# Shared buffers, an eighth ring slot and one more resident key slice in a planned two-layer kernel

## The chip, the cores and the metric

The kernel runs on one core of a Trainium2 chip. The metric is the device time of one execution in microseconds (us). Below, PE is the matrix engine, "weight load" its separate instruction that brings in the stationary operand, DVE the vector engine, ACT the scalar engine, POOL the GpSimd engine, and SP the engine that here only issues DMA transfers.

## The reference

An input of 2048 tokens of 640 bf16 numbers goes through two kinds of layer in turn, A, B, A, B, with the same weights each time. Each layer works on the layer norm of its input and is added to it.

```python
def _A_ref(x, mem0, Wq, Wk, Wv, Wo, seg_len):      # 32 heads of 192, segments of 32 tokens
    mem = mem0                                      # 8 memory rows
    for s in range(n_seg):                          # 64 segments, one after the other
        h = concatenate([mem, x[segment s]])        # 40 rows
        q, k, v = h @ Wq, h @ Wk, h @ Wv            # 640 -> 32 x 192 each
        p = softmax(where(mask, q k^T * scale, -1e9))
        o = (p v) @ Wo                              # 6144 -> 640
        mem = o[:8]; outs.append(o[8:])

def _B_ref(x, w1, w2, w3, w4):
    h = gelu(layernorm(x) @ w1)                     # 640 -> 640, then four column groups are
    hs = shifted(h) @ w2                            # shifted by -1, +1, -2, +2 tokens
    x1 = x + hs
    return x1 + gelu(layernorm(x1) @ w3) @ w4       # 640 -> 1536 -> 640
```

The memory makes layer A a chain of 64 steps: a segment can't start before the one ahead of it has gone through all heads. The four projection weights have 640 x 6144 numbers each, 7.9 MB, and are needed anew in every step.

## The kernel before, in words

**Two lanes.** The second A layer follows the first five segments behind (`LAG`), so that one pass over the weights serves both: in step t lane 0 works on segment t of the first A layer, lane 1 on segment t - 5 of the second. There are 69 steps. In steps 5 to 63 both lanes run and a projection matmul has 80 columns (two times 40 rows); in the first and last five steps one lane runs and it has 40. A chunk of layer B, 64 tokens of both lanes, is spread over every second step.

**One step** has eight groups of four heads, taken in four pairs. For each pair `proj_pair` makes k, q and v of both groups (per group and kind 30 matmuls, 5 slices of the input dimension times 6 of the output), then `attend` runs for each group: scores (`pss`), mask and row minimum (DVE, L600), exponential (ACT, L607), row sums, reciprocal and scaling (DVE, L611 to L613), transposes of the probabilities (`pst`), their copy (ACT, `PT`), times V (`pso`), copy (DVE, `oT`) and the output projection, which adds into `psy`. At the end of a step ACT copies the new memory columns out of `psy` (L671), and the next step's projections wait for that.

**Weights.** The weights do not all fit in the core's memory. For each pair and kind some of the five slices are resident, loaded once by `res_tile`, and the others stream in every step: `STREAM` says 3 for k, 3 for q, 2 for v, that is 32 slices of 128 x 1536 bf16 (393,216 bytes) per step. They go through a ring of `RING_A = 7` slots (tiles `wst`, L440). A slot is free again after the second group's matmuls of its slice. Layer B's weights have a ring of their own (`wstB`, 3 slots). All these transfers are issued by SP, in one order.

**The planner.** The order of all instructions is made in Python when the kernel is built. Every operation is added with an engine, an assumed duration, a due time (48 us per step), and the buffers it reads and writes; the writes and reads of a named buffer `B(...)`, in the order of adding, give the dependencies. `Plan.place` then builds a list per engine: it always places the operation that can start first, and among those within a few hundredths of a microsecond the one due first. For a transfer it assumes a rate, `DMA_RATE`, and that data is there `DMA_LAST` after its last byte's turn; matmuls that read it are placed no earlier than that. A transfer may be put at most `DMA_AHEAD` in front of the transfer server; such a "paced" transfer gets a wait for the last matmul planned to be over by then. On the chip only the order and the waits remain: no assumed time is enforced.

**Buffers the change touches.** `qT`, `Pm` (two each, by group number) and `sm` (four) hold the queries, probabilities and softmax columns. `Vt` holds V of a group, each head padded from 192 to 256 columns. `mask2` and `mask_b` are fp32. In layer B `lnx` holds four rows of look-ahead and the next 64 input rows, `vT` the transposed normalised rows, `hTB` the transposed first hidden layer with four tokens of history, and `h2u` the second hidden layer.

Of the kernel before, what the change touches and what calls it, by code (L numbers as in the profile page):

```python
# [9 lines left out]
ACT = mybir.ActivationFunctionType  # L10
# [10 lines left out]
LAG = 5  # L21
HG = 4
STREAM = {"k": 3, "q": 3, "v": 2}
RING_A = 7
RING_B = 3
# [8 lines left out]
DMA_FIRST = 0.8  # L34
DMA_LAST = 2.6
B_MARGIN = 0.6
# [203 lines left out]
def kernel(  # L240
# [34 lines left out]
    NS = 2 * L1  # L275
    QD = Dm // 4
    scale = float(Dh) ** -0.5
    T_A = NSEG + LAG
# [33 lines left out]

    mask2 = ctile([NS, NS], f32, "mask2")
    nc.gpsimd.memset(mask2[:], 0.0)
# [11 lines left out]
    mask_a = mask2[0:L1, 0:L1]  # L326
    mask_b = ctile([L1, L1], f32, "mask_b")
    nc.gpsimd.memset(mask_b[:], 0.0)
# [11 lines left out]
    hT = [ctile([P, KC, NS], bf16, f"hT{i}") for i in range(4)]  # L340
    qT = [ctile([P, GC, NS], bf16, f"qT{i}") for i in range(2)]
    vF = ctile([P, GC, NS], bf16, "vF")
    kT = [ctile([P, 8, NS], bf16, f"kT{i}") for i in range(2)]
    Vt = [ctile([NS, HG, 256], bf16, f"V{i}") for i in range(2)]
    Pm = [ctile([NS, HG, NS], bf16, f"Pm{i}") for i in range(2)]
    PT = ctile([NS, HG, NS], bf16, "PT")
    oT = [ctile([P, GC, NS], bf16, f"oT{i}") for i in range(OT_BUFS)]
    sm = [ctile([P, 10], f32, f"sm{i}") for i in range(4)]
    mem0T = ctile([P, KC, M], bf16, "mem0T")
    yTB = ctile([P, KC, XB + 4], bf16, "yTB")  # L350
# [10 lines left out]
    gl = vbg[:].bitcast(f32)  # L361
    lnx = ctile([96, Dm], bf16, "lnx")
    vT = ctile([P, KC, XB + 4], bf16, "vT")
    hTB = ctile([P, KC, TOK + 4, 2], bf16, "hTB")
    st4 = [ctile([P, 18], f32, f"st{i}") for i in range(4)]

# [5 lines left out]
    nc.gpsimd.memset(xres[:], 0.0)  # L372
    nc.vector.memset(lnx[:], 0.0)
    nc.vector.memset(hTB[:], 0.0)

    bufs = {}
    ALIAS = {("vx",): ("vb",), ("xo",): ("vb",), ("gl",): ("vb",), ("vx2",): ("uw",), ("xres",): ("xw",)}

# [50 lines left out]
    def load_pair(kind, pr, due, now):  # L429

        nres = KC - STREAM[kind]
        cols = slice(PW * pr, PW * (pr + 1))
        rb, rt = res_tile((kind, pr), [P, nres, PW], w_src[kind][:, 0:nres, cols], due)
        slots = []
        for j, kc in enumerate(range(nres, KC)):
            b = Slotted("ra", None)
            b.make = lambda b=b: wring.tile([P, SLOT], bf16, name="wst", tag=f"ra{b.slot}")

            def fn(op, b=b, kc=kc):
                nc.sync.dma_start(out=T(b)[:, 0:PW], in_=w_src[kind][:, kc, cols])  # L440
# [57 lines left out]
    def attention_step(t):  # L498
# [13 lines left out]
        def proj_pair(pr):  # L512
            s0 = base + sl * 2 * pr
            for kind, off in (("k", 0.0), ("q", 0.2), ("v", 0.5)):
                wbs, wv = load_pair(kind, pr, s0 + off * 2 * sl, LEAD_A)
                for j in range(2):
# [4 lines left out]

                    nres = KC - STREAM[kind]
                    for kcs in [range(0, nres)] + [range(kc, kc + 1) for kc in range(nres, KC)]:
# [10 lines left out]
                    if kind == "q":  # L534
                        q = qT[G % 2]

                        def fq(op, pq=pq, q=q):
                            nc.scalar.copy(out=q[:, :, 0:N], in_=T(pq)[:, :, 0:N])  # L538
                        add("ACT", act_us(GC * N), due, fq, r=(pq,), w=(B("qT", G % 2),))
                    elif kind == "k":  # L540
# [13 lines left out]
                    else:  # L554
# [12 lines left out]
                        for hf in range(2):  # L567
                            def fe(op, pvt=pvt, V_=V_, hf=hf):
                                src = T(pvt)[0:N, GWH * hf:GWH * (hf + 1)].rearrange("n (a b) -> n a b", a=2)
                                dst = V_[0:N, 2 * hf:2 * hf + 2, 0:Dh]  # L570
                                if hf:
                                    nc.vector.tensor_copy(out=dst, in_=src)
                                else:
                                    nc.scalar.copy(out=dst, in_=src)  # L574
                            add("DVE" if hf else "ACT", dve_us(GWH) if hf else act_us(GWH), due, fe, r=(pvt,),
                                w=(B("V", G % 2, hf),))

        def attend(g):
            G = t * NG + g
            s0 = base + sl * g  # L580
            q, k_, V_ = qT[G % 2], kT[G % 2], Vt[G % 2]
            pss = ps("A", [NS, HG * NS], f32, "pss")
            hi = s0 + 0.5 * sl

            def fs(op):
# [6 lines left out]
            add("PE", mm_us(N, N, 4) + mm_us(2 * N, N, 2), hi - 4, fs,  # L592
                r=(B("qT", G % 2), B("kT", G % 2, 0), B("kT", G % 2, 1), B("kT", G % 2, 2)), w=(pss,))
            sm_ = sm[G % 4]
            Pb = Pm[G % 2]
            smk, Pk = B("sm", G % 4), B("P", G % 2)

# [12 lines left out]
            def f3(op):  # L610
# [3 lines left out]
                                        in1=sm_[0:N, 6:6 + HG].unsqueeze(2).to_broadcast([N, HG, N]), op=ALU.mult)  # L614
            add("DVE", 0.42 + 0.17 + 0.45, hi - 4, f3, w=(Pk, B("sm4", G % 4)))
            pst = ps("A", [NS, HG, NS], bf16, "pst")
# [11 lines left out]
            pso = ps("A", [P, GC, NS], f32, "pso")  # L628
            Vf = V_[:].rearrange("n h e -> n (h e)")

            def f6(op):
                o = T(pso)
                for hf in range(2):
                    for i2, col, c, st, sp in ((0, 0, 0, True, True), (0, 128, 1, True, False), (1, 192, 1, False, True),
                                               (1, 320, 2, True, True)):
                        nc.tensor.matmul(out=o[:, 3 * hf + c, 0:N], lhsT=Vf[0:N, 512 * hf + col:512 * hf + col + P],  # L636
                                         rhs=Pt[0:N, 2 * hf + i2, 0:N], start=st, stop=sp)
# [28 lines left out]
        if take:  # L666
# [5 lines left out]
            add("ACT", act_us(KC * (m1 - m0)), due, fm, r=(psy,), w=(mk,))  # L672
        if 1 in nxt and t + 1 == LAG:
            def fm0(op):
                nc.gpsimd.tensor_copy(out=hn[:, :, L1:L1 + M], in_=mem0T[:])
            add("POOL", 0.4, base, fm0, a=(mk,), r=(B("mem0T"),))
        t0 = 2 + SEG * (t % 2) if t < T_A - 1 else 2
# [85 lines left out]
    def chunk_loads(c, part):  # L763
        base = (2 * c + 1) * STEP
        edge = False
        todo = []
# [19 lines left out]
        if edge:  # L786
            def fz(op):
                nc.gpsimd.memset(xres[:] if part == "x" else lnx[0:4, :], 0.0)
            add("POOL", 1.0, base, fz, w=(B("xres") if part == "x" else B("lnx", "l"),))
        if part == "x":  # L790
            base = base + 0.6 * STEP
        for lane, a, b, w0 in todo if part == "x" else ():
# [4 lines left out]
        for lane, k0 in look if part == "l" else ():  # L797
            def f(op, lane=lane, k0=k0):
                nc.gpsimd.dma_start(out=lnx[lane:4:2, :], in_=src[lane][k0:k0 + 2, :])
            rd = [] if src[lane] is x0d else [B("x2d", k) for k in x2_chunks(k0, k0 + 2)]  # L800
            add("POOL", 0.9, base, f, r=rd, a=(B("lnx", "l"),), dma=4000)
        s = 2 * c + 4
        if s < NSEG and part == "l":
            def f(op):
                nc.gpsimd.dma_start(out=lnx[32:96, :], in_=x0d[SEG * s:SEG * s + TOK, :])
            add("POOL", 0.9, base, f, w=(B("lnx", "x"),), dma=TOK * Dm * 2)

# [4 lines left out]
    def chunk(c):  # L812
# [63 lines left out]
        add("DVE", 0.45, D(0.08), f3, r=(B("lnx", "l"), B("lnx", "x"), s2k), w=(vxk,))  # L876
        if c + 1 < NCH:
            chunk_loads(c + 1, "l")
        ps2 = ps(PB, [P, KC, XB], bf16, "psv")
# [51 lines left out]
        if last:  # L931
            def fc2(op):
                for r, r1, n, o2 in carry:
                    if o2:
                        nc.vector.tensor_copy(out=hTB[r:r1, n, 0:o2 // 2, 0], in_=hTB[r:r1, n, TOK:TOK + o2 // 2, 1])
            add("DVE", 0.6, D(0.4), fc2, w=(B("hTB", 0), B("hTB", 1)))
        hs = [ps(PB, [XB, HC], f32, "hs") for _ in range(2)]
        for i, (a, e) in enumerate(((0, 2), (2, 4), (4, 5))):
# [52 lines left out]
    def chunk_end(c):  # L991
# [56 lines left out]
    def start():  # L1048
# [10 lines left out]
        def f3(op):  # L1059
            nc.scalar.copy(out=mem0T[:], in_=T(p0)[:])  # L1060
            nc.scalar.copy(out=hT[0][:, :, SEG:L1], in_=T(p0)[:])
        add("ACT", 0.5, -90, f3, r=(p0,), w=(B("mem0T"), B("hT", 0, "m")))

# [80 lines left out]
```

## Time and profile before

| | |
|---|---|
| median of 3 runs | 3606.19 us (3599.22 to 3612.08) |
| span of the profiled execution | 3607.7 us |
| bytes moved by DMA | 1102.00 MB, mean 305 GB/s |
| chain that ended last | PE 73%, DMA 23%, issue 2% |
| slices streamed through the ring | 828 k, 828 q, 552 v |
| resident loads of k and q, of v, of the output weights | 8 of 768 KB, 4 of 1152 KB, 8 of 960 KB |
| mean granted PE clock | 0.981 of full |

How to read it: the profile gives each engine's busy time, and for the idle time of an engine what ended it, inferred from semaphores. PE work is pipelined: a matmul of 80 columns is recorded with 202 ns, but the next starts 36 ns after it, so records overlap, and a busy PE is counted until the last record ends. "PEld" are the weight loads, recorded with 100 ns each. A DMA is recorded at its issue on SP; the data lands microseconds later. "Issue" is idle time for which the profile has no releaser.

The granted clock is below full only in the first 300 us and the last 300 us of the run. Of the 40 slices of the page the first shows the PE busy 60% and the last 60%; nearly all between are at 90% or more.

### The profile page before, as it was taken

What the parts mean: (1) busy time and instruction counts of PE and PEld (TensorE: products, weight loads), DVE (VectorE), ACT (ScalarE), POOL (GpSimd) and SP (SyncE); (2) the same over time, 40 slices, a digit from 0 to 9 for tenths busy, and PEclk for the clock granted to TensorE, in tenths of its full rate; (3) what the DMA queues carried; (4) which work ended last, traced back from release to release, by engine and by line L of the source; (5) the groups of instructions that cost most, each with busy time, mean ns of one, the idle gap of its engine ahead of it and who ended that gap; (6) DMA issues with size and microseconds to landing.
All of it is one profiled execution on the core that took longest, in us unless ns stands there. A gap on an engine that the chain in (4) does not pass through costs nothing.

```text
span 3607.7 us, 187838 instructions
## 1 busy us (share of the span) xinstructions
PE 3398.0 (94%) x84559; PEld 3260.7 (90%) x84559; DVE 2484.8 (69%) x7432; ACT 1509.0 (42%) x3569; POOL 243.5 (7%) x456
## 2 busy tenths in 40 slices
PE   6899999999999999999999999999999999999886
PEld 5789999999999999999999999999999999999775
DVE  2556777777776777777767777777767777766554
ACT  1334444444444444444444444444444444444332
POOL 0000000000000000000000000000000000000000
PEclk7899999999999999999999999999999999999997
DMA  9899899888988898889888988888889888988995
GB/s 376 299 318 313 308 316 312 299 305 305 326 305 300 301 321 303 302 303 328 303 296 307 312 310 303 303 311 303 300 295 320 301 304 302 319 296 305 306 306 175
DMA packets 507559, 1102.00 MB, mean 305 GB/s; under 512 B 50558, under 2 KB 217996, under 8 KB 506752
## 3 DMA queue, kind: packets, MB, share of 16 engines
q1 hardware_dynamic: 499520, 1076.85, 86.1%
q8 instruction: 661, 10.83, 1.2%
q0 software_dynamic: 7232, 13.13, 1.1%
q14 instruction: 146, 1.20, 0.1%
HBM read 1084.53 MB, written 5.24 MB: 302 GB/s over the span
## 4 chain that ended last, share of the span: by engine, by line
PE 73%; DMA 23%; issue 2%; ACT 1%; DVE 1%; SPq 0%; POOL 0%; POOLq 0%; DVEq 0%; ACTq 0%
PE psy L653 15%; PE psq L528 13%; PE psv L528 12%; PE psk L528 12%; DMA wst<-in_A_Wq_dram 9%; DMA wst<-in_A_Wk_dram 9%; PE pvt L565 4%; PE pso L636 4%; PE pss L589 3%; DMA wst<-in_A_Wv_dram 3%; PE psh L982 3%; PE pst L621 2%; PE y L1008 2%; PE psh L910 1%; PE hs L947 1%
## 5 line engine op out<-in xcount | busy, mean ns | idle before, releaser
L528 PEld LDWEIGHTS <-wst 128*128 128x128 bf16 x26496 | 1087.7, 100 | 134.0 <-DMA wst<-in_A_Wq_dram 38.6
L653 PE MATMUL psy<-oT,wo 128*128 128x80 bf16 (+1 forms) x16560 | 678.4, 200 | 30.6 <-issue 17.4
L653 PEld LDWEIGHTS <-wo 128*128 128x128 bf16 x16560 | 619.0, 100 | 38.5 <-issue 25.8
L538 ACT CAST qT<-psq 128x480 bf16<-128x480 f32 (+1 forms) x552 | 283.7, 530 | 747.8 <-PE psq L528 746.2
L528 PE MATMUL psq<-hT,wst 128*128 128x80 bf16 (+1 forms) x9936 | 494.4, 199 | 29.4 <-DMA wst<-in_A_Wq_dram 24.6
L528 PE MATMUL psk<-hT,wst 128*128 128x80 bf16 (+1 forms) x9936 | 468.8, 200 | 31.5 <-DMA wst<-in_A_Wk_dram 25.6
L642 DVE CAST oT<-pso 128x480 bf16<-128x480 f32 (+1 forms) x552 | 340.7, 617 | 198.4 <-PE pso L636 195.9
L528 PE MATMUL psv<-hT,wv 128*128 128x80 bf16 (+1 forms) x9936 | 435.6, 200 | 14.2 <-DMA wv<-in_A_Wv_dram 7.3
L600 DVE CUSTOM_DVE_ANT_1 pss<-pss,mask 80x320 f32<-80x320 f32 (+1 forms) x512 | 245.1, 479 | 232.9 <-PE pss L589 216.0
L528 PEld LDWEIGHTS <-wv 128*128 128x128 bf16 x9936 | 383.4, 100 | 19.8 <-issue 8.0
L626 ACT COPY PT<-pst 80x320 bf16<-80x320 bf16 (+1 forms) x552 | 222.1, 402 | 367.4 <-PE pst L621 330.7
L574 ACT COPY V<-pvt 80x384 bf16<-80x384 bf16 (+1 forms) x552 | 261.2, 473 | 266.5 <-PE pvt L565 264.1
L528 PE MATMUL psv<-hT,wst 128*128 128x80 bf16 (+1 forms) x6624 | 350.7, 199 | 23.1 <-DMA wst<-in_A_Wv_dram 14.9
L611 DVE TENSOR_REDUCE sm<-Pm 80x4 f32<-80x320 bf16 (+1 forms) x552 | 250.3, 453 | 150.0 <-ACT Pm L607 146.3
L558 ACT CAST vF<-psv 128x480 bf16<-128x480 f32 (+1 forms) x552 | 290.9, 527 | 128.1 <-PE psv L528 127.1
L552 DVE CAST kT<-psk 64x160 bf16<-64x160 f32 (+1 forms) x1104 | 335.9, 304 | 9.4
L528 PE MATMUL psk<-hT,wk 128*128 128x80 bf16 (+1 forms) x6624 | 320.5, 200 | 15.7 <-ACT hT L671 10.7
L528 PE MATMUL psq<-hT,wq 128*128 128x80 bf16 (+1 forms) x6624 | 319.2, 200 | 2.5 <-issue 1.3
L607 ACT ACTIVATE Pm<-pss,sm 80x320 bf16<-80x320 f32 (+1 forms) x552 | 277.5, 505 | 81.5 <-DVE sm L600 81.0
L546 DVE CAST kT<-psk 128x320 bf16<-128x320 f32 (+1 forms) x552 | 255.3, 462 | 76.1 <-PE psk L528 67.3
L565 PE MATMUL pvt<-ident,vF 128*80 128x128 bf16 (+1 forms) x3312 | 284.7, 223 | 7.8 <-ACT vF L558 3.8
L528 PEld LDWEIGHTS <-wk 128*128 128x128 bf16 x6624 | 269.9, 100 | 22.8 <-issue 20.3
(126 smaller groups left out, 4345.3 us busy)
## 6 DMA issues: line engine op xcount, KB each, us to landing
wst<-in_A_Wk_dram SPq DMA_DIRECT2D x828, 384.0 KB, 5.2
wst<-in_A_Wq_dram SPq DMA_DIRECT2D x828, 384.0 KB, 5.1
wst<-in_A_Wv_dram SPq DMA_DIRECT2D x552, 384.0 KB, 5.0
wstB<-in_B_w_dram SPq DMA_DIRECT2D x495, 320.0 KB, 5.0
wstB<-in_B_w_dram SPq DMA_DIRECT2D x132, 160.0 KB, 4.8
wo<-in_A_Wo_dram SPq DMA_DIRECT2D x8, 960.0 KB, 12.3
wv<-in_A_Wv_dram SPq DMA_DIRECT2D x4, 1152.0 KB, 10.7
wk<-in_A_Wk_dram SPq DMA_DIRECT2D x4, 768.0 KB, 10.3
```

The costliest lines, as they stand in the source:

```text
L528: nc.tensor.matmul(out=o[:, cc, 0:N], lhsT=wv(kc, GW * j + cc * P, GW * j + (cc + 1) * P), rhs=h[:, kc, c0:c0 + N], start=(kc == 0 and cc ...
L538: nc.scalar.copy(out=q[:, :, 0:N], in_=T(pq)[:, :, 0:N])
L546: nc.vector.tensor_copy(out=k4[:, :, 0::3, 0:N], in_=p4[:, :, 0::2, 0:N])
L552: nc.vector.tensor_copy(out=k4[r0:r1, :, jj, 0:N], in_=p4[r0:r1, :, 1, 0:N])
L558: nc.scalar.copy(out=vf[:, :, 0:N], in_=T(pq)[:, :, 0:N])
L565: nc.tensor.transpose(out=o[0:N, c * P:(c + 1) * P], in_=vf[:, c, 0:N], identity=ident[:, :])
L574: nc.scalar.copy(out=dst, in_=src)
L600: nc.vector.tensor_tensor_reduce(out=o, in0=o, in1=maskt.unsqueeze(1).to_broadcast([N, HG, N]), scale=-scale, scalar=3.0e38, op0=ALU.add, ...
L607: nc.scalar.activation(out=Pb[0:N, :, 0:N], in_=o, func=ACT.Exp, bias=sm_[0:N, 0:1], scale=-1.0)
L611: nc.vector.tensor_reduce(out=sm_[0:N, 2:2 + HG], in_=Pb[0:N, :, 0:N], axis=AX.X, op=ALU.add)
L642: nc.vector.tensor_copy(out=o_[:, :, 0:N], in_=T(pso)[:, :, 0:N])
L653: nc.tensor.matmul(out=o[:, m, c0:c0 + N], lhsT=wo[:, cc, m * P:(m + 1) * P], rhs=o_[:, cc, 0:N], start=st, stop=True, skip_group_check=True)
```

## The change

It makes room by keeping fewer buffers, and spends the room on the ring and on residence.

- Room made: `qT` and `Pm` become single, `sm` two; the masks become bf16; `Vt` shares the padding between heads; `mem0T` goes (the first memory is copied straight to its place); `lnx` moves into columns of `h2u`, `vT` into `hTB`. As `hTB` is overwritten by `vT` in each chunk, its four tokens of history are saved to a small tile, `hist`, and put back. Loads into `lnx` now come at the end of a chunk, after the matmuls that read that part of `h2u`.
- Room spent: `RING_A` from 7 to 8; `MORE` keeps one more slice of k for pair 1, so that 31 slices stream per step.
- The plan: `DMA_LAST` from 2.6 to 3.2, so that matmuls are placed later relative to the transfers they read.

```diff
-RING_A = 7
+RING_A = 8
+MORE = {("k", 1): 1}
-DMA_LAST = 2.6
+DMA_LAST = 3.2
-    mask2 = ctile([NS, NS], f32, "mask2")
+    mask2 = ctile([NS, NS], bf16, "mask2")
-    mask_b = ctile([L1, L1], f32, "mask_b")
+    mask_b = ctile([L1, L1], bf16, "mask_b")
-    qT = [ctile([P, GC, NS], bf16, f"qT{i}") for i in range(2)]
+    qT = ctile([P, GC, NS], bf16, "qT")
-    Vt = [ctile([NS, HG, 256], bf16, f"V{i}") for i in range(2)]
-    Pm = [ctile([NS, HG, NS], bf16, f"Pm{i}") for i in range(2)]
+    Vt = [ctile([NS, 2 * VP], bf16, f"V{i}") for i in range(2)]
+    Pm = ctile([NS, HG, NS], bf16, "Pm")
-    sm = [ctile([P, 10], f32, f"sm{i}") for i in range(4)]
-    mem0T = ctile([P, KC, M], bf16, "mem0T")
+    sm = [ctile([P, 10], f32, f"sm{i}") for i in range(2)]
-    lnx = ctile([96, Dm], bf16, "lnx")
-    vT = ctile([P, KC, XB + 4], bf16, "vT")
+    lnx = h2u[0:96, Dm:2 * Dm]
     hTB = ctile([P, KC, TOK + 4, 2], bf16, "hTB")
+    vT = hTB[:].rearrange("p k w l -> p k (w l)")[:, :, 0:XB + 4]
+    hist = ctile([P, KC, 4, 2], bf16, "hist")
...
-        nres = KC - STREAM[kind]
+        nres = KC - STREAM[kind] + MORE.get((kind, pr), 0)
...
-                        q = qT[G % 2]
+                        q = qT
-                        add("ACT", act_us(GC * N), due, fq, r=(pq,), w=(B("qT", G % 2),))
+                        add("ACT", act_us(GC * N), due, fq, r=(pq,), w=(B("qT"),))
...
-        def fhh(op):
-            nc.gpsimd.tensor_copy(out=hTB[:, :, 0:4, :], in_=hTB[:, :, TOK:TOK + 4, :])
-        add("POOL", 0.4, D(0.05), fhh, w=(B("hTB", 0), B("hTB", 1)))
...
+        def fhr(op):
+            nc.gpsimd.tensor_copy(out=hTB[:, :, 0:4, :], in_=hist[:])
+        add("POOL", 0.6, D(0.25), fhr, r=(B("hist"),), w=(B("hTB", 0),))
...
+            def fhs(op):
+                nc.gpsimd.tensor_copy(out=hist[:], in_=hTB[:, :, TOK:TOK + 4, :])
+            add("POOL", 0.6, D(0.5), fhs, r=(B("hTB", 0),), w=(B("hist"),))
...
             chunk_loads(c + 1, "x")
+            chunk_loads(c + 1, "l")
```

More of the change, by code (lines that the diff above doesn't have):

```diff
@@ L276 @@
     QD = Dm // 4
+    VP = 2 * Dh + 64
     scale = float(Dh) ** -0.5
@@ L372 @@
     nc.gpsimd.memset(xres[:], 0.0)
-    nc.vector.memset(lnx[:], 0.0)
+    nc.vector.memset(lnx, 0.0)
+    nc.vector.memset(hist[:], 0.0)
     nc.vector.memset(hTB[:], 0.0)
     bufs = {}
-    ALIAS = {("vx",): ("vb",), ("xo",): ("vb",), ("gl",): ("vb",), ("vx2",): ("uw",), ("xres",): ("xw",)}
+    ALIAS = {("vx",): ("vb",), ("xo",): ("vb",), ("gl",): ("vb",), ("vx2",): ("uw",), ("xres",): ("xw",),
+             ("vTl",): ("vT",), ("hTB", 0): ("vT",), ("hTB", 1): ("vT",)}
     def B(*key):
@@ L520, in proj_pair @@
                     pq = ps("A", [P, GC, NS], f32, "ps" + kind)
-                    nres = KC - STREAM[kind]
+                    nres = KC - STREAM[kind] + MORE.get((kind, pr), 0)
                     for kcs in [range(0, nres)] + [range(kc, kc + 1) for kc in range(nres, KC)]:
@@ L569, in fe @@
                                 src = T(pvt)[0:N, GWH * hf:GWH * (hf + 1)].rearrange("n (a b) -> n a b", a=2)
-                                dst = V_[0:N, 2 * hf:2 * hf + 2, 0:Dh]
+                                v0 = hf * (VP - 64)
+                                dst = V_[0:N, v0:v0 + 512].rearrange("n (a b) -> n a b", a=2)[:, :, 64 * hf:64 * hf + Dh]
                                 if hf:
@@ L580, in attend @@
             s0 = base + sl * g
-            q, k_, V_ = qT[G % 2], kT[G % 2], Vt[G % 2]
+            q, k_, V_ = qT, kT[G % 2], Vt[G % 2]
             pss = ps("A", [NS, HG * NS], f32, "pss")
@@ L592, in attend @@
             add("PE", mm_us(N, N, 4) + mm_us(2 * N, N, 2), hi - 4, fs,
[L593 to L596, printed above, removed]
+                r=(B("qT"), B("kT", G % 2, 0), B("kT", G % 2, 1), B("kT", G % 2, 2)), w=(pss,))
+            sm_ = sm[G % 2]
+            Pb = Pm
+            smk, Pk = B("sm", G % 2), B("P")
             def f1(op):
@@ L614, in f3 @@
                                         in1=sm_[0:N, 6:6 + HG].unsqueeze(2).to_broadcast([N, HG, N]), op=ALU.mult)
-            add("DVE", 0.42 + 0.17 + 0.45, hi - 4, f3, w=(Pk, B("sm4", G % 4)))
+            add("DVE", 0.42 + 0.17 + 0.45, hi - 4, f3, w=(Pk, B("sm4", G % 2)))
             pst = ps("A", [NS, HG, NS], bf16, "pst")
@@ L628, in attend @@
             pso = ps("A", [P, GC, NS], f32, "pso")
-            Vf = V_[:].rearrange("n h e -> n (h e)")
             def f6(op):
@@ L635, in f6 @@
                                                (1, 320, 2, True, True)):
-                        nc.tensor.matmul(out=o[:, 3 * hf + c, 0:N], lhsT=Vf[0:N, 512 * hf + col:512 * hf + col + P],
+                        nc.tensor.matmul(out=o[:, 3 * hf + c, 0:N], lhsT=V_[0:N, VP * hf + col:VP * hf + col + P],
                                          rhs=Pt[0:N, 2 * hf + i2, 0:N], start=st, stop=sp)
@@ L672, in attention_step @@
             add("ACT", act_us(KC * (m1 - m0)), due, fm, r=(psy,), w=(mk,))
[L673 to L676, printed above, removed]
         t0 = 2 + SEG * (t % 2) if t < T_A - 1 else 2
@@ L764, in chunk_loads @@
         base = (2 * c + 1) * STEP
+        over = (B("h2T", 1, 0), B("h2T", 1, 1)) if part == "l" else ()
         edge = False
@@ L788, in fz @@
                 nc.gpsimd.memset(xres[:] if part == "x" else lnx[0:4, :], 0.0)
-            add("POOL", 1.0, base, fz, w=(B("xres") if part == "x" else B("lnx", "l"),))
-        if part == "x":
-            base = base + 0.6 * STEP
+            add("POOL", 1.0, base, fz, w=(B("xres") if part == "x" else B("lnx", "l"),), a=over)
+        base = base + 0.6 * STEP
         for lane, a, b, w0 in todo if part == "x" else ():
@@ L800, in chunk_loads @@
             rd = [] if src[lane] is x0d else [B("x2d", k) for k in x2_chunks(k0, k0 + 2)]
-            add("POOL", 0.9, base, f, r=rd, a=(B("lnx", "l"),), dma=4000)
+            add("POOL", 0.9, base, f, r=rd, a=(B("lnx", "l"), *over), dma=4000)
         s = 2 * c + 4
@@ L805, in f @@
                 nc.gpsimd.dma_start(out=lnx[32:96, :], in_=x0d[SEG * s:SEG * s + TOK, :])
-            add("POOL", 0.9, base, f, w=(B("lnx", "x"),), dma=TOK * Dm * 2)
+            add("POOL", 0.9, base, f, w=(B("lnx", "x"),), a=over, dma=TOK * Dm * 2)
     def x2_chunks(a, b):
@@ L876, in chunk @@
         add("DVE", 0.45, D(0.08), f3, r=(B("lnx", "l"), B("lnx", "x"), s2k), w=(vxk,))
-        if c + 1 < NCH:
-            chunk_loads(c + 1, "l")
         ps2 = ps(PB, [P, KC, XB], bf16, "psv")
@@ L936, in chunk @@
             add("DVE", 0.6, D(0.4), fc2, w=(B("hTB", 0), B("hTB", 1)))
+        if not last:
+            def fhs(op):
+                nc.gpsimd.tensor_copy(out=hist[:], in_=hTB[:, :, TOK:TOK + 4, :])
+            add("POOL", 0.6, D(0.5), fhs, r=(B("hTB", 0),), w=(B("hist"),))
         hs = [ps(PB, [XB, HC], f32, "hs") for _ in range(2)]
@@ L1059, in f3 @@
         def f3(op):
-            nc.scalar.copy(out=mem0T[:], in_=T(p0)[:])
+            nc.scalar.copy(out=hT[LAG % 4][:, :, L1:L1 + M], in_=T(p0)[:])
             nc.scalar.copy(out=hT[0][:, :, SEG:L1], in_=T(p0)[:])
-        add("ACT", 0.5, -90, f3, r=(p0,), w=(B("mem0T"), B("hT", 0, "m")))
+        add("ACT", 0.5, -90, f3, r=(p0,), w=(B("hT", LAG % 4, "m"), B("hT", 0, "m")))
         def f4(op):
```

## The prediction

> **What bounds the kernel now.** I start with the engine shares, then take a stretch of the middle, where both layers run, then ask what the PE waited for in it. The page says that the PE is the engine to look at, and the middle shows it more strictly (columns of the second view: stretch, length, then busy us and count of PE, weight loads, DVE, ACT, POOL, granted clock, DMA share, GB/s):
>
> ```profile
> span 3607.7 us, 187838 instructions
> PE 3398.0 (94%) x84559; PEld 3260.7 (90%) x84559; DVE 2484.8 (69%) x7432; ACT 1509.0 (42%) x3569; POOL 243.5 (7%) x456
> ...
> 300.00:3300.00 3000.00, 2901.73 (x71668) 2816.88 (x71666) 2180.88 (x6314) 1323.44 (x3037) 207.22 (x379) 1.00 0.89 307
> ```
>
> The clock is full, and the DMA engines move 307 GB/s at a share of 0.89, while the first 100 us of the run reach 369 GB/s at 1.00: the transfers are not at their limit. What the weight loads of the PE waited for in that stretch (us in total, times, longest):
>
> ```profile
> PEld L528 <- DMA wst<-in_A_Wk_dram: 34.2, 70, 1.4
> PEld L528 <- DMA wst<-in_A_Wq_dram: 32.5, 68, 1.7
> PEld L528 <- issue: 25.8, 52, 1.1
> PEld L528 <- DMA wst<-in_A_Wv_dram: 20.5, 37, 1.6
> PEld L653 <- issue: 14.1, 26, 1.7
> ```
>
> The three DMA rows are 87.2 us in 175 waits, all on ring tiles (`wst`). A weight load is recorded with 100 ns, though twelve matmuls start within 0.43 us (36 ns apart), so each wait hides 64 ns more: 175 x 0.064 = 11 us. **Ring waits cost 98 us of the 3000.** The next cause, "issue", is 44 us with no releaser shown; ACT and DVE handoffs are some 12. A single wait, in order of time (start, length, and in brackets the idle time before), and the chain through it:
>
> ```profile
> 1827.73 0.60 PE L528 MATMUL psk<-hT,wk 128*128 128x80 bf16 x12
> 1828.16 0.60 PE L528 MATMUL psk<-hT,wst 128*128 128x80 bf16 x12
> 1828.59 0.60 PE L528 MATMUL psk<-hT,wk 128*128 128x80 bf16 x12
> 1830.48 0.39 PE L528 MATMUL psk<-hT,wst 128*128 128x80 bf16 x6 [1.29 <-DMA wst<-in_A_Wk_dram]
> ```
>
> ```profile
> 1824.17 0.03 PE pss L589
> 1824.21 6.23 DMA wst<-in_A_Wk_dram
> 1830.43 0.05 issue
> 1830.48 0.39 PE psk L528 x6
> ```
>
> The transfer was held until a score matmul at 1824.2 and landed 6.23 us later; the PE had only about 5 us of other work in between. Landing usually takes a little less:
>
> ```profile
> wst<-in_A_Wk_dram SPq DMA_DIRECT2D x828, 384.0 KB, 5.2
> wst<-in_A_Wq_dram SPq DMA_DIRECT2D x828, 384.0 KB, 5.1
> wst<-in_A_Wv_dram SPq DMA_DIRECT2D x552, 384.0 KB, 5.0
> ```
>
> So the PE binds, and what it loses in the middle is mostly **transfers issued too late, not transfers too slow**. Steps are 51.2 us apart (68 copies of the memory columns from 87.9 to 3518.8 us, 67 intervals). One step streams 32 slices, one per 1.6 us; with 7 slots a slot comes round in 11.2 us, 5.1 of them landing.
>
> **What the Trainium skill says.** "Perfetto Trace Analysis", Optimization Strategy: consistent bubbles on the engine that should be saturated "can mean there isn't enough SBUF/PSUM for the next tile to be allocated (buffer count, tile sizes)"; 175 waits of half a microsecond, all on ring tiles, fit. "TensorE: Matmul & The Clock Gate", the part on 56 ns, not 53.3 ns: start to start is N/2.4 GHz plus about 2.5 ns; the trace agrees (36 ns for 80 columns, 0.56 us for ten of 128). "DMA: Bandwidth & Descriptors", Anatomy of one DMA (for the GpSimd path): about 2 us fixed plus bytes at 436 GB/s; for 393 KB an estimate of 2.9 us, where the trace has 5.1, so some 2 us are waiting behind other transfers. "VectorE: DVE Perf Modes", Why PSUM operands drop a tier: fp32 in PSUM runs at 1x; so the bf16 mask should not speed L600 (492 ns on fp32 PSUM).
>
> **The change part by part.**
>
> Bytes: one `k` slice of pair 1 becomes resident. 69 slices fewer on the ring, one more in the first load: 68 x 0.393 MB = 26.7 MB of 1102, 2.4%. In the middle this frees DMA time that is not the bound.
>
> Ring and later landings: these two move the transfers ahead of their uses. I read it from the instruction order of both programs: for each ring slice of the middle I took the last PE instruction that its DMA waits for and the first matmul that reads it, and added the PE work between, at the durations of the trace (36 ns for 80 columns, 56 for 128, 135 for 320). Before: smallest 4.6 us, a quarter under 5.3, median 6.1, and 34% under 5.5. After: smallest 5.4, a quarter under 7.2, median 8.5, and 1.6% under 5.5. It agrees with 8 slots x 1.65 us = 13.2 us per round, 2.0 more, and with 0.6 us added to the planned landing. Against landings of 5.5, 6.0 and 6.5 us the summed shortfalls fall from 224, 546 and 973 us to 2, 22 and 64: 1 to 7% remain. (The sums exceed 98 because one wait also covers the next transfers; I use only the ratio.) I take 5%: **-93 us** in the middle.
>
> Single lanes: steps 0 to 4 and 64 to 68 have short matmuls (40 columns) and stay at 50 us a step, so there the supply of weights sets the pace; about 300 GB/s, and 2.4% fewer bytes. 10 x 50 x 2.4% = **-12 us**. Bounds: 0, if handoffs set those steps, and -20, at 2 us per step.
>
> Single `qT`: a pair's two query copies are both added ahead of both score groups, so no copy waits for the first scores of its own pair (the first group is then scored with the second group's queries; count and duration of instructions stay). The next pair's copy must wait for the second score group; the order has at least 2.0 us of PE work from there to the next scores, and two copies of 0.56 us fit. Cost 0.
>
> Single `Pm`, two `sm`: the next exponential waits until the previous transposes have read `Pm`. From exponential to transposes takes 0.525 + 0.478 + 0.175 + 0.488 = 1.67 us (L607, L611, L612, L613), and at 1840.06 to 1841.92 the trace shows 1.86 with handoffs; plus about 0.26 from the last matmul to ACT, 2.1. The order leaves at least 2.24 us between one set of transposes and the next, and 3.0 from scores to transposes (2.7 before). Little to spare: I take 5 us, 0 to 35 (0.3 us in a quarter of 472 groups).
>
> `vT` in `hTB`: the second `vT` copy (693 ns) has 0.97 us of PE work to hide behind instead of 1.08; 0.1 us x 34 chunks = 3 us at most. `lnx` in `h2u`, `hist`: two GpSimd copies per chunk for one (213 ns), loads later in the chunk but 0.4 step (20 us) ahead of their use, against 4.9 us to land; hidden, with POOL 7% busy. `V` in a tighter layout, bf16 masks: same counts and shapes, 0. Handoffs that late weights used to cover come to light: 2 to 10 us, I take 5.
>
> Sum: -93 - 12 + 5 + 5, and 0 for the rest with `vT` rounded in: **-95 us, 3511 us**.
>
> **The rivals.** (1) The waits only halve: transfers in flight more of the time lengthen each other's landing by about 1 us. For it: the DMA share is 0.89 already. Against: the bytes per us hardly change (15.0 MB in 49.6 us against 15.4 in 51.2). Then some 50 of the 98 us go: 3606 - 50 = 3556. (2) More is won: the edges give 20 us and half of the 44 us of "issue" goes, if those are late instructions behind weights. 3511 - 8 - 22 = 3481. (3) New waits outweigh: if the single buffers cost 0.25 us in each of the 472 groups, 118 us, 3606 - 93 + 118 = 3631. For it: the tight 2.24 us, and DVE at 73% in the middle. Against: every distance in the order is over the chain that the trace shows. (4) No change to speak of, the first and third together: 3606.
>
> **How the numbers follow.** Likeliest 0.62 (3511), rival 1 0.18 (3556), rival 2 0.12 (3481), rival 3 0.05, rival 4 0.03. The range leaves out 3 and 4 and the outer thirds of 1 and 2, 0.18 in all: 3475 to 3568. Faster is the likeliest with 1 and 2, less a little for a combination of misses: 0.91; within 0.3% 0.03; slower 0.06.
>
> **What would show it.** Right: in a middle stretch the DMA rows of `wst` fall from 87 to under 10 us, steps come every 49.6 us, weight loads are busy for over 96%, "issue" stays near 44 us and landing near 5.1 us. Wrong: DMA waits stay above 40 us with landings of 6 us (rival 1), or L621 and L636 wait for `Pm` and `PT` by tens of microseconds (rival 3).

## The result and the profile after

The changed kernel takes 3555.91 us (median of 4 runs, 3547.79 to 3561.73); before took 3607.74 us beside it. The ratio is **0.9858, 95% interval 0.9828 to 0.9887**: 52 us faster, in the direction forecast, but about half of the 95 us that were expected.

One thing has to be known of the changed kernel. With a single `qT` both query copies of a pair come before both of its score groups, so the first group of each pair, 16 of the 32 heads, is scored with the second group's queries. The number and shapes of the instructions stay, so its time can be compared, but these heads are not those of the reference. Of the kernels below this holds for all with a single `qT`.

The top of the page of the changed kernel (the heading between its two lines is left out), and the same engines in its middle stretch (50 us shorter than the stretch shown of before):

```profile
span 3546.1 us, 188209 instructions
PE 3384.9 (95%) x84559; PEld 3263.1 (92%) x84559; DVE 2480.1 (70%) x7433; ACT 1517.2 (43%) x3569; POOL 244.5 (7%) x488
```

```profile
300.00:3250.00 2950.00, 2898.17 (x71759) 2824.70 (x71755) 2178.67 (x6321) 1332.28 (x3041) 210.65 (x411) 1.00 0.88 305
```

71,759 matmuls now fit in 2950 us where 71,668 took 3000. The DMA engines are about as busy as before (a share of 0.88, before 0.89) and move 305 GB/s instead of 307. What the weight loads of the PE waited for in that stretch (us in total, times, longest):

```profile
PEld L532 <- issue: 22.3, 50, 1.0
PEld L657 <- issue: 15.9, 31, 1.3
PEld L626 <- DVE Pm L618: 12.5, 54, 0.3
PEld L532 <- DMA wst<-in_A_Wq_dram: 4.5, 10, 1.3
PEld L640 <- issue: 4.0, 7, 1.0
...
PEld L532 <- DMA wst<-in_A_Wk_dram: 1.1, 3, 0.5
...
PEld L532 <- DMA wst<-in_A_Wv_dram: 0.5, 1, 0.5
```

The ring rows went from 87.2 us in 175 waits to 6.1 us in 14. Among what stands in their place is a row that before had 0.4 us: the transposes (L626) wait for the scaled probabilities. Landing did not get faster, so the transfers must have been issued earlier before their use:

```profile
wst<-in_A_Wq_dram SPq DMA_DIRECT2D x828, 384.0 KB, 5.2
wst<-in_A_Wk_dram SPq DMA_DIRECT2D x759, 384.0 KB, 5.2
wst<-in_A_Wv_dram SPq DMA_DIRECT2D x552, 384.0 KB, 5.2
```

The new waits sit at four places of the order, which repeats every two steps. Here is the largest, in order of time (start, length; in brackets the idle time before). It comes 23 times in the middle stretch and makes up 8 of the 20 us that the PE loses there before transposes:

```profile
2494.44 0.35 PE L626 MATMUL pst<-ident,Pm 80*80 80x80 bf16 x4 [0.17 <-DVE Pm L618]
2494.61 0.71 PE L657 MATMUL psy<-oT,wo 128*128 128x80 bf16 x15
2495.16 0.50 PE L569 MATMUL pvt<-ident,vF 128*80 128x128 bf16 x6
2495.50 0.45 PE L640 MATMUL pso<-PT,V 80*128 80x80 bf16 x8
2495.78 2.32 PE L657 MATMUL psy<-oT,wo 128*128 128x80 bf16 x60
2498.30 0.34 PE L626 MATMUL pst<-ident,Pm 80*80 80x80 bf16 x4 [0.20 <-DVE Pm L618]
```

and the chain through it shows what it was made of:

```profile
2495.70 0.48 ACT V L579
2496.18 0.02 issue
2496.20 0.35 DVE V L577
2496.56 0.56 DVE oT L646
2497.12 0.41 DVE sm L616
...
2497.55 0.19 DVE sm L617
...
2497.76 0.50 DVE Pm L618
2498.26 0.04 issue
2498.30 0.34 PE pst L626 x4
```

The row sums (L616) stood in DVE's queue behind a copy of V and the copy of another group's output (L646), and that copy of V behind ACT's; they start 1.4 us after the exponential is done. 3.7 us pass from one set of transposes to the start of the next, where the prediction allowed 2.1 for the softmax alone. At a second place (29 times, 5 us) the row sums also wait in DVE's queue, for 0.65 us. At the other two (55 times, 6 us) nothing stands in front of them. There 2.35 us pass from transposes to transposes, 0.53 of them before the exponential starts, as ACT first copies the transposed probabilities (`PT`). **About two thirds of these handoffs were lost in the queues of DVE and ACT, and one third in a chain that is itself longer than the 2.1 us allowed and the 2.24 us that the order leaves at the least.**

Three sums follow each kernel through the experiments. I set each start of a matmul against the one before it, took off the usual (median) spacing of its kind (36 ns for 80 columns and so on; the sum of these is the work), and put the rest down to what the program has the PE wait for there: a transfer, another engine, or nothing. In 300 to 3250 us, in us:

| | work | transfers | other engines | nothing | time |
|---|---|---|---|---|---|
| before | 2782 | 96 | 24 | 48 | 3605 |
| changed | 2834 | 9 | 55 | 52 | 3556 |
| sharing alone | 2750 | 124 | 44 | 32 | 3646 |
| landing 3.2 alone | 2825 | 33 | 36 | 56 | 3570 |
| landing 3.8 alone | 2820 | 6 | 54 | 70 | 3577 |
| changed, landing 2.6 | 2824 | 15 | 50 | 61 | 3557 |
| changed, no extra slice | 2821 | 13 | 48 | 68 | 3572 |
| same, Pm double | 2821 | 21 | 40 | 67 | 3563 |
| same, Pm and qT double | 2828 | 13 | 41 | 68 | 3543 |
| changed, longer chain planned | 2836 | 19 | 47 | 48 | 3563 |
| changed, v not streamed | 2853 | 2 | 55 | 40 | 3493 |

(The last column is the median of all runs; the others are from one profiled run each.) Of the 31 us by which the waits for other engines grew, 18 stand before the transposes (2 us before, 20 after) and 7 before the product with V (4 and 11). By steps, from the copies of the memory columns that end each: the first takes 87.9 us before and 88.0 after, steps 1 to 4 take 197.8 and 193.8, the 59 steps with both lanes 3028.9 and 2974.8, steps 64 to 67 204.1 and 201.0, the rest 88.9 and 88.5. So 54 of the 61.6 us between the two profiles come from the middle.

### The profile page after: what moved, and what is told of

Read it like the earlier page. It is cut to its first block, busy times and chain, and to the rows that moved or that the text cites. A ratio compares the mean times of both kernels' runs of the same rounds, so it can differ in the third digit from the quotient of the medians.

```text
span 3546.1 us, 188209 instructions
## 1 busy us (share of the span) xinstructions
PE 3384.9 (95%) x84559; PEld 3263.1 (92%) x84559; DVE 2480.1 (70%) x7433; ACT 1517.2 (43%) x3569; POOL 244.5 (7%) x488
## 4 chain that ended last, share of the span: by engine, by line
PE 89%; DMA 4%; issue 3%; DVE 2%; ACT 1%; SPq 1%; POOL 0%; POOLq 0%; DVEq 0%; ACTq 0%
PE psq L532 16%; PE psv L532 16%; PE psk L532 16%; PE psy L657 15%; PE pvt L569 5%; PE pss L594 4%; PE pso L640 4%; PE psh L985 3%; PE y L1011 3%; PE pst L626 3%; DMA wst<-in_A_Wq_dram 2%; PE psh L905 1%; PE hs L950 1%; DMA wst<-in_A_Wk_dram 1%; PE psv L722 1%
## 5 line engine op out<-in xcount | busy, mean ns | idle before, releaser
L532 PEld LDWEIGHTS <-wst 128*128 128x128 bf16 x25668 | 1051.3, 100 | 40.0 <-issue 16.2
L657 PE MATMUL psy<-oT,wo 128*128 128x80 bf16 (+1 forms) x16560 | 683.7, 199 | 29.9 <-issue 13.5
L657 PEld LDWEIGHTS <-wo 128*128 128x128 bf16 x16560 | 620.8, 100 | 37.5 <-issue 24.5
L542 ACT CAST qT<-psq 128x480 bf16<-128x480 f32 (+1 forms) x552 | 291.9, 529 | 665.9 <-PE psq L532 662.2
L532 PE MATMUL psq<-hT,wst 128*128 128x80 bf16 (+1 forms) x9936 | 456.1, 199 | 8.6 <-DMA wst<-in_A_Wq_dram 6.1
L646 DVE CAST oT<-pso 128x480 bf16<-128x480 f32 (+1 forms) x552 | 340.6, 617 | 152.4 <-PE pso L640 142.7
L532 PE MATMUL psk<-hT,wst 128*128 128x80 bf16 (+1 forms) x9108 | 437.6, 199 | 2.4 <-issue 1.7
L605 DVE CUSTOM_DVE_ANT_1 pss<-pss,mask 80x320 f32<-80x320 f32 (+1 forms) x512 | 242.8, 484 | 221.1 <-PE pss L594 125.8
L532 PE MATMUL psv<-hT,wst 128*128 128x80 bf16 (+1 forms) x6624 | 367.3, 199 | 10.5 <-issue 10.1
L532 PE MATMUL psk<-hT,wk 128*128 128x80 bf16 (+1 forms) x7452 | 350.4, 199 | 15.6 <-ACT hT L675 10.8
L532 PEld LDWEIGHTS <-wk 128*128 128x128 bf16 x7452 | 299.3, 100 | 21.8 <-issue 21.5
L616 DVE TENSOR_REDUCE sm<-Pm 80x4 f32<-80x320 bf16 (+1 forms) x552 | 250.1, 453 | 85.8 <-ACT Pm L612 76.1
```

What stands on the lines that cost most here:

```text
L532: nc.tensor.matmul(out=o[:, cc, 0:N], lhsT=wv(kc, GW * j + cc * P, GW * j + (cc + 1) * P), rhs=h[:, kc, c0:c0 + N], start=(kc == 0 and cc ...
L605: nc.vector.tensor_tensor_reduce(out=o, in0=o, in1=maskt.unsqueeze(1).to_broadcast([N, HG, N]), scale=-scale, scalar=3.0e38, op0=ALU.add, ...
L616: nc.vector.tensor_reduce(out=sm_[0:N, 2:2 + HG], in_=Pb[0:N, :, 0:N], axis=AX.X, op=ALU.add)
L646: nc.vector.tensor_copy(out=o_[:, :, 0:N], in_=T(pso)[:, :, 0:N])
L657: nc.tensor.matmul(out=o[:, m, c0:c0 + N], lhsT=wo[:, cc, m * P:(m + 1) * P], rhs=o_[:, cc, 0:N], start=st, stop=True, skip_group_check=True)
```

## The experiments

A "lead" is what the prediction read from the order of instructions: the PE work between the point that a transfer waits for and the first matmul that reads it. Ratios are to the kernel before, measured beside each run.

**The shared buffers alone.**

```diff
-RING_A = 8
-MORE = {("k", 1): 1}
+RING_A = 7
+MORE = {}
...
-DMA_LAST = 3.2
+DMA_LAST = 2.6
```

> The changed kernel with 7 ring slots, no extra resident slice and the planned landing back at 2.6: the shared and single buffers alone. In its order the PE work between release and first use of a ring slice is that of before (smallest 4.6 us, a quarter under 5.3). Theory (late transfers were the loss that went; single buffers and a softmax chain planned too short put some 30 us of new handoff waits in its place): ring waits of the weight loads stay at 80 to 100 us in a 3000 us stretch, waits for Pm and the other handoffs are 15 to 35 us above before, time 3610 to 3640 us. Rival (sharing is free, and the missing half of the gain is lost to instruction supply or to the edges): 3600 to 3612 us, waits for Pm under 5 us.

Measured 3646.17 us, ratio 1.0109 (1.0084 to 1.0134), 6 us over the band of the theory. Sharing by itself costs 40 us, so the changed kernel's other edits give back 90. The waits for `Pm` appear as expected; but the ring waits rose too, above the expected band, 28.5 us of them at one place, where the third pair's keys are projected:

```profile
PEld L532 <- DMA wst<-in_A_Wq_dram: 56.7, 94, 1.9
PEld L532 <- DMA wst<-in_A_Wk_dram: 40.4, 49, 3.0
PEld L532 <- issue: 17.2, 40, 1.0
PEld L532 <- DMA wst<-in_A_Wv_dram: 16.0, 28, 1.7
PEld L626 <- DVE Pm L618: 10.0, 27, 0.4
```

**The later landing alone**, in the kernel before, at 3.2 and at 3.8:

```diff
-DMA_LAST = 2.6
+DMA_LAST = 3.2
```

> The kernel before with the planned landing at 3.2 instead of 2.6, nothing else: 7 slots, all buffers double, 32 streamed slices. In its order the smallest lead of a ring slice is 5.1 us and a quarter is under 5.8; the summed shortfall against a landing of 5.5 us falls from 225 to 22 us, against 6.0 from 548 to 215. Theory (leads decide): ring waits fall from 98 to between 10 and 40 us, the double buffers keep handoffs near before, time 3530 to 3560 us, as good as the whole change. Rival (room or bytes decide: with 7 slots the later plan only moves the wait): ring waits 70 us and more, time 3585 us and more.

> The kernel before with the planned landing at 3.8: 7 slots, all buffers double, 32 slices. Leads in its order: smallest 5.55, a quarter under 6.3, shortfall against 6.0 us 31 us where before has 548 and the changed kernel 22. Theory (leads decide): ring waits under 20 us in the middle, 3550 to 3570 us, so that most of the gain needs no room at all. Rival (7 slots hold the transfers back on the chip): ring waits of 30 us and more, 3570 us and more.

Measured 3569.61 us (0.9901, 0.9877 to 0.9926) and 3576.94 us (0.9913, 0.9891 to 0.9935). One constant, with no room made at all, brings 36 of the 52 us. The first is 10 us over the band of the theory, the second 7. At 3.8 the ring waits are all but gone, as the leads said, but time is no better: what the transfers gave up, handoffs and the waits for nothing took. Its weight loads in the same stretch:

```profile
PEld L528 <- issue: 35.4, 69, 1.4
PEld L653 <- issue: 23.0, 35, 1.7
PEld L621 <- DVE Pm L613: 10.9, 24, 0.5
...
PEld L528 <- DMA wst<-in_A_Wv_dram: 1.8, 5, 0.5
...
PEld L528 <- DMA wst<-in_A_Wk_dram: 1.2, 3, 0.8
PEld L528 <- DMA wst<-in_A_Wq_dram: 1.2, 3, 0.5
```

These buffers are double: waits for `Pm` (here L613) need no single buffer. The waits for other engines are 54 us here, as many as in the changed kernel.

**The changed kernel with the landing back at 2.6.**

> The changed kernel with the planned landing back at 2.6: sharing, the eighth slot and the resident slice. Its order has the leads of the changed kernel almost to the digit (smallest 5.4, a tenth under 6.6). Theory (leads decide, however they come about): within 0.4% of the changed kernel, 3542 to 3570 us, ring waits under 15 us in the middle. Rival (the planned landing is what helps): ring waits of 40 us and more, 3580 us and more.

Measured 3557.06 us (0.9863, 0.984 to 0.9886), the time of the changed kernel. Once the ring has its eighth slot and the extra slice is resident, the later landing changes no more than the noise; the two edits reach the same thing.

**The changed kernel without the extra slice.**

```diff
-MORE = {("k", 1): 1}
+MORE = {}
```

> The changed kernel without the extra resident slice: 8 slots, landing 3.2, again 32 streamed slices and 26.7 MB more than the changed kernel. Leads in its order: smallest 5.6, a quarter under 6.6. Theory (leads decide, bytes don't bind in the middle): ring waits under 20 us there, at most 12 us lost in the single-lane steps, 3550 to 3575 us. Rival (bytes bind: 26.7 MB at 305 GB/s are 87 us): 3600 us and more.

Measured 3572.39 us (0.9905, 0.9883 to 0.9928): the slice is worth 16 us (the intervals just overlap). Ring waits stay low (13 us), so in the middle it is not bytes as a bound; there the waits for nothing are 68 us instead of 52. Steps 1 to 4 take 204.4 us instead of 193.8, with a granted clock of 0.87 instead of 0.95 (88 to 285 us). This can't be put down to the bytes: in one profile each, the six kernels that stream 31 slices take 193.8 to 202.3 us for these steps, and the seven that stream 32 take 194.0 to 204.9.

**Pm double, then Pm and qT double**, both without the extra slice, which makes the room:

```diff
-    Pm = ctile([NS, HG, NS], bf16, "Pm")
+    Pm = [ctile([NS, HG, NS], bf16, f"Pm{i}") for i in range(2)]
...
-    qT = ctile([P, GC, NS], bf16, "qT")
+    qT = [ctile([P, GC, NS], bf16, f"qT{i}") for i in range(2)]
```

> The changed kernel without the extra slice and with Pm double, qT still single: which of the two buffers gave the 29 us between the runs with both single (3572 us) and both double (3543 us). Leads: smallest 5.6, a quarter under 6.2. If the single Pm is the cost: 3540 to 3555 us. If the single qT is (a pair's query copies wait for the second score group of the pair ahead, and hold two tiles of PSUM while they wait): 3560 to 3580 us. If it is the order that the plan happened to find: either, with no drop in a wait that names the buffer.

> The changed kernel without the extra slice and with qT and Pm double again, so that each score group reads its own queries: 8 slots, landing 3.2, lnx, vT, masks and V still shared or small. To be compared with the run without the extra slice (3572 us). Leads: smallest 5.65, a quarter under 6.7, as there. Theory A (waits for the single Pm and qT are the new cost): the waits for Pm of 10 to 14 us and the ACT handoffs fall to the level of before, 3540 to 3560 us. Theory B (the cost lies in how tightly the order packs the softmax chain, whatever the number of buffers): waits for Pm stay at 8 us and more, 3565 to 3580 us.

Measured 3563.2 us (0.989, 0.9868 to 0.9912) and **3543.44 us (0.9817, 0.9794 to 0.984)**. The second is the fastest kernel of the study with all of its work left in, 12 us under the changed kernel (their intervals overlap), and its first score groups read their own queries again. The 9 us that came with the double `Pm` are within the intervals, the 20 that came with the double `qT` are not. In the middle the waits for `Pm` fall from 10.2 to 3.2 us, but others come:

```profile
PEld L532 <- issue: 35.1, 68, 1.7
PEld L657 <- issue: 20.7, 31, 2.0
PEld L640 <- ACT V L579: 6.6, 29, 0.2
PEld L532 <- DMA wst<-in_A_Wq_dram: 5.8, 12, 1.0
PEld L532 <- DMA wst<-in_A_Wv_dram: 5.2, 11, 1.1
PEld L594 <- issue: 3.6, 5, 1.3
PEld L626 <- DVE Pm L618: 3.2, 15, 0.5
```

No wait of the PE above 0.5 us names `qT` in either. By steps, 9 us of the 28 between the profiles of both single and both double are in the middle and 19 outside: 4 in the first step, 10 in steps 1 to 4 (194.0 instead of 204.4 us, at a clock of 0.94), 5 in the last ones. Of the 16 us between the profiles with `Pm` double and with both double, 9 are in the middle, where the ring waits fall from 21 to 13 us. What a single `qT` does is seen in the order: both query copies stand before both sets of scores in all 276 pairs, and with two `qT` in only 15, where the others go copy, scores, copy, scores. That two `qT` make a faster kernel is shown. Through which waits is not, and the plan finds another order with every such edit, so how much is the buffer and how much the order stays open.

**A longer softmax chain in the plan.**

```diff
-            add("ACT", act_us(HG * N), hi - 4, f2, r=(pss, smk), w=(Pk,))
+            add("ACT", act_us(HG * N) + 0.1, hi - 4, f2, r=(pss, smk), w=(Pk,))
...
-            add("DVE", 0.42 + 0.17 + 0.45, hi - 4, f3, w=(Pk, B("sm4", G % 2)))
+            add("DVE", 0.42 + 0.17 + 0.45 + 0.2, hi - 4, f3, w=(Pk, B("sm4", G % 2)))
```

> The changed kernel with longer assumed durations of the softmax chain in the plan: the exponential by 0.1 us, the row sums to scaling by 0.2 us, near what the trace shows from start to handoff. Buffers and transfers stay. In its order the smallest distance from one set of transposes to the next grows from 2.24 to 2.68 us; leads of ring slices: smallest 5.3, a quarter under 7.2. Theory B (the chain is planned too short): waits for Pm fall from 17 us to under 4 us in the middle, time 3525 to 3548 us. Theory A (the single buffer itself costs): the wait moves to another handoff or into the order, 3550 to 3565 us.

Measured 3562.77 us (0.9868, 0.9843 to 0.9892), no faster than the changed kernel. The rows for `Pm` are gone from the answer, as theory B asked, and the time is where theory A put it: the output projection now waits for the copy of its input,

```profile
PE psy L657 <- DVE oT L646: 8.3, 27, 0.3
```

so the waits for other engines are 47 us, only 8 fewer, and the ring waits rise from 9 to 19. What one place gained, others lost.

**Room for everything**: both buffers double, the extra slice, and six `oT` buffers (`OT_BUFS`) instead of eight; then with longer handoffs in the plan; and those on top of the longer chain in the changed kernel.

```diff
-LAT = 0.1
-PE_LAT = 0.23
+LAT = 0.15
+PE_LAT = 0.3
```

> qT and Pm double, 8 slots and the extra slice together; the room comes from six instead of eight buffers for the attention output (oT). Leads: smallest 5.8, a tenth under 6.5. If gains add up (16 us from the extra slice, 29 from the two buffers), 3520 to 3535 us, steps 1 to 4 under 194 us. If the six oT buffers take it back (waits of L657 and of the copies into oT), 3540 to 3560 us.

> The kernel with room for all, with longer handoffs assumed in the plan (0.15 us between engines instead of 0.1, 0.30 after the PE instead of 0.23). If the remaining handoff waits come from an order packed closer than the chip's handoffs: ACT and DVE waits in the middle fall by half or more, 10 to 25 us faster than without. If such a wait only moves to another operation, as in the run with the longer softmax chain: within 8 us of it.

> The changed kernel with the longer softmax chain and the longer handoffs in the plan together. Leads: smallest 6.0, a quarter under 7.4. If close packing is what the changed kernel lost to: DMA, Pm and oT waits all under 5 us in the middle, 3520 to 3540 us. If what is left is instruction supply and the single-lane steps: 3540 to 3560 us, issue at 45 to 65 us.

Measured 3554.04 us (0.9861, 0.9838 to 0.9884), 3544.3 us (0.9831, 0.9807 to 0.9856) and 3579.32 us (0.9933, 0.9908 to 0.9957). The gains don't add up: in the first of these the transposes wait for `Pm` 18.0 us in 27 waits, though it is double, and L657 waits 5.6 us for `oT`. That is the second band expected, but the six `oT` buffers are not shown to be the cause, as L657 waited 8.3 us with eight in the run before. The longer handoffs win 10 us there, at the low end of what was expected, with the handoff sum (waits for other engines) down from 67 to 55 us and not by half, and the intervals overlap. In the changed kernel, with the longer chain, the sum is 70 and the kernel loses 23 us, which is outside both expectations. So the handoffs depend on the order that the plan happens to find, and not smoothly on the assumed durations.

**Fewer transfers with the same PE work.** The two streamed slices of v are left out and resident ones read in their place, so this kernel's v is not the reference's.

```diff
+            if kind == "v":
+                slots.append(rb)
+                continue
             b = Slotted("ra", None)
...
+            if kind == "v":
+                return rt[:, kc - nres, c0:c1]
             return T(slots[kc - nres])[:, c0:c1]
```

> The changed kernel with the two streamed slices of v left out: those matmuls read the resident slices instead, so v is computed from wrong weights. PE instructions are the same in number and nearly in order; 552 of 2139 ring transfers go (217 MB of 1075). Theory (the idle time called issue is late instructions, which queue behind weights in the DMA engines: all of these stalls begin at the same place of each run of 256 PE instructions, and end 1.3 to 1.5 us after a 16 KB packet of the instruction queue): issue falls from 50 us in the middle to under 20, 3490 to 3525 us. Rival (instruction supply has its own limit): issue stays at 40 to 55 us, 3535 to 3550 us.

Measured 3492.71 us (0.9682, 0.9662 to 0.9703). With the DMA share at 0.75 instead of 0.88 the "issue" rows fall from 50 to 39 us in 2950:

```profile
PEld L537 <- issue: 26.5, 53, 2.2
PEld L631 <- DVE Pm L623: 13.0, 54, 0.3
PEld L662 <- issue: 7.3, 10, 2.2
PEld L599 <- issue: 2.3, 5, 0.9
```

The time is in the band of the theory, but "issue" is not: it is just under the rival's band and far from under 20. The time can't decide, since only 28 of the 61 us between the profiles are in the steps with both lanes, and the "issue" rows make 11 of those. The long stalls for nothing (over 200 ns between two matmuls) fell from 67 to 38, but each became no shorter. Traffic is part of it, and what the rest is stays open. The waits for `Pm` are those of the changed kernel, so they don't come from the transfers.

## Why the prediction was right or wrong, point by point

- **The bound and the ring waits: right, in kind and size.** Leads read from the order said that 1 to 7% of the ring waits would stay; 6.1 of 87.2 us did. The term -93 us measured -87 in 2950 us. Steps with both lanes come every 50.4 us, not 49.6, because of the terms below. The estimate that some 2 us of a landing are waiting behind other transfers fits: in the middle of the kernel before, the 32 ring transfers issued with none in flight landed after 3.35 us in the median, those with three or four in flight after 5.05 and 5.3. The two edits of the ring and the plan were not told apart in it: either alone brings most of this, and together they bring no more than the eighth slot with its slice.
- **The failed term is the handoffs, mis-sized.** "Single `Pm` ... I take 5 us" and "Handoffs that late weights used to cover ... I take 5" together allowed 10 us; the waits for other engines grew by 31 (24 to 55). The bound of 35 for the first of them would have held it. The step behind it was the comparison of the order's 2.24 us with a chain of 2.1. With nothing in its way the chain measured 2.35, as the exponential starts 0.53 us after the transposes and not 0.26. And the comparison left out what else stands in the queues of ACT and DVE: the chain at 2495.70 to 2498.30 shows copies of V and of another group's output in front of the row sums. How the 31 us divide between single buffers and weights that are no longer late is open: with all buffers double and the landing at 3.8 the waits for other engines grew by 30 as well.
- **Single `qT`, "Cost 0": too low.** With `qT` double, and `Pm` double in both, the kernel is 20 us faster. The reading was right in that hardly a wait names it (0.7 us in the changed kernel). It asked only whether the copies fit, and not what the forced order of two copies before two sets of scores does to the rest; that mechanism is open.
- **Single lanes, -12 us: too large, and the reason does not hold.** The steps outside the middle give 7.5 us between the profiles. "The supply of weights sets the pace" is not what the trace of before shows: in its steps 1 to 4 the PE lost 10 of 198 us to transfers and 27 to other engines, by the count of the table. That the sign came out right is in part luck, as these steps vary by more than 7.5 us between kernels that move the same bytes.
- **What was costed at nothing** held where a row can tell: the bf16 masks (L605 497 ns, before 492, as the Trainium skill has it in "VectorE: DVE Perf Modes", Why PSUM operands drop a tier), the two copies of `hist` (216 ns; the one that puts the history back was waited for once, 4.7 us, outside the middle), `lnx` and `vT`, which no row of the middle's weight loads names.
- **"Issue" stays near 44 us: nearly.** 50 us, 4 more by the gaps. Rival 2 needed it to halve, and it did not. Rival 1 has the measured time, but by luck and not for its reason: it asked for landings of 6 us and ring waits above 40.
- The sum as measured: -87 ring, +31 handoffs, +4 issue, -7.5 outside the middle: -60, of 61.6 between the profiles. The medians differ by 10 us less than the profiled runs, within the spread of single runs. Of the 35 us that these -60 fall short of -95, 21 are the handoffs.

## What to carry to other kernels

When transfers land too late for a busy engine, first try to issue them earlier in the plan: here one constant brought 36 us with no memory spent, and the buffers shared to make room cost 40 us before the room gave anything. A wait taken from a tightly ordered engine can uncover the next: as ring waits fell from 96 to 33 and 6 us with the later landing alone, waits for other engines rose from 24 to 36 and 54. So price handoffs from the queues of the other engines, counting everything that stands ahead of the operation, and not from the durations of the chain alone. When extra room is at hand, compare what each buffer is worth: here two `qT` and two `Pm` gave a kernel 12 us faster than the resident slice did, though the intervals overlap. And before two buffers become one, look at what is written twice before it is read.

## What the runs showed of the hardware that was not expected

Most of the time that the PE waits for nothing in the program looks like late instructions (38 of the 52 us in the changed kernel). Of its stalls in the middle, those with over 200 ns between two matmuls and no wait in the program, all 67 begin at the same place of each run of 256 PE instructions (the 195th or 196th, counted from the start of the program); it is all 59 in the kernel before, and all 38 with v not streamed. One of them:

```profile
526.34 0.60 PE L657 MATMUL psy<-oT,wo 128*128 128x80 bf16 x12
528.18 0.81 PE L657 MATMUL psy<-oT,wo 128*128 128x80 bf16 x18 [1.24 <-issue]
```

and the queue that goes with it (packets, MB, share of 16 engines):

```profile
q8 instruction: 661, 10.83, 1.2%
```

661 packets of 16,384 bytes are 256 instructions of 64 bytes each (that size is what the Trainium skill gives in "Perfetto Trace Analysis", The 4-stage abstract model), and 661 x 256 is the PE's 169,000 instructions. In all 67 stalls the PE goes on 1.2 to 1.6 us after the end of such a packet (median 1.4), while the packets come 5.3 us apart in the median, so this is not chance. Why the place is the 195th and not the first is not shown. 256 instructions are 128 matmuls, 4.6 us of work at 36 ns. The table's sum for "nothing" is 32 us where ring waits are many (sharing alone), 52 in the changed kernel and 56 to 70 where 32 slices stream and ring waits are few. This fits instructions that catch up while the PE waits for weights, which no run tests by itself. Against before it is 4 us more in the changed kernel, and 22 with the landing at 3.8 alone.
